# The second expert layer with its paired row blocks computed transposed, 256 tokens at a time

## The chip, the cores and the metric

The kernel runs on one core of one Trainium2 chip. The metric is the device time of one execution in microseconds (us), as the median of several runs. TensorE (PE in the profile) does the matrix products, ScalarE (ACT) and VectorE (DVE) read and write on-chip tiles elementwise, GpSimd (POOL) issues the gathers and scatters of rows, and SyncE (SP) issues the other transfers.

## What is computed

Attention with a window of 128 and 4 sink keys feeds two mixtures of experts. The change lies in the second one, cut here from the reference:

```python
logits = x @ w_gate                        # x 1536 x 512, 8 experts
expert_idx = np.argmax(logits, axis=1)
gate_w = softmax(logits)[arange(N), expert_idx]
for e in range(E):
    mask = expert_idx == e
    xe = x[mask]
    h = np.maximum(xe @ w1[e], 0.0)        # w1[e] 512 x 1024
    ye = h @ w2[e]                         # w2[e] 1024 x 512
    out[mask] = gate_w[mask, None] * ye
```

Every row goes to one expert, which is known only at run time. All products are made of parts: a number is split into a rounded high part and the remainder (low part), and one product is the sum of three matmuls, low x high, high x low, high x high (`mm3`, L66).

## The kernel before

Attention and the first mixture come first. The second mixture is cut into **items**, each a block of rows of one expert, numbered in the order in which they run. Items 0 and 1 are the two blocks of the fullest expert; they run while the tables for the others are still being made. Then follow 16 items: five **pairs** (3,4), (6,7), (9,10), (12,13), (15,16), two blocks of 128 rows of the same expert, and six **singles** 2, 5, 8, 11, 14, 17, of another expert each. Item 2 has 128 rows; singles 5 to 17 have 64 rows at most (`HALF`), put with their low parts side by side into 128 columns so that two matmuls do instead of three (`mm`, L768).

An item needs four weight tiles of 1 MB: halves 0 and 1 of the first layer (`w1`) and of the second (`w2`). A pair shares its four. So there are 11 x 4 = 44 tiles after item 1. Each is loaded by SP into one of four raw buffers and **split** in two pieces (`w_split`, L163): per piece ScalarE rounds 128x1024 elements into the high part (L175) and VectorE subtracts (L177). The split tiles go round seven slots (`SLOTS`, L136: wha0, wha1, xh0, xh1, xh2, whb0, whb1 and the same with l for the low parts) in the order of `SEQ` (L127): first layer of an item, second layer of the item before it, and so on. `spend(n)` (L849) writes n pieces into the program where it is called, if a slot is free; `ensure` (L863) writes what is still missing of a tile right before the matmuls that use it; `used` (L868) marks a slot free.

What an item i does:

- `gather(i)`: POOL fetches its rows by index. `xs_trans(i)` (L750): four transposes on PE, then the high part by ScalarE and the low part by VectorE.
- `m2_l1(i, hf)` (L781), the first layer's half hf: activations stationary, 512 weight columns moving, so the result has rows on the partitions. 12 matmuls of 512 columns a half (8 for a `HALF` item), then the result goes out through the rectifier (ScalarE for half 0, VectorE for half 1). A `HALF` item sums its two parts there (`both`, L776: a copy on ScalarE, an addition on VectorE).
- `h_trans(i)` (L800): eight transposes on PE turn the hidden layer, so that it can be stationary in the second layer; ScalarE makes the high part (L819) and VectorE the low part (L820).
- `m2_l2(i)` (L823): 24 matmuls of 512 columns (16 for a `HALF` item), then scaling by the gate on ScalarE (L840; for a `HALF` item `both` comes ahead of it) and a scatter of rows by POOL (L841).

The order is written out by hand in the loop at L1510: the first layer of item i+1 (with `gather` and `xs_trans` of later items), then the second layer of item i, with `h_trans(i+1)` in its middle. Each engine works off its own list in order; an instruction that waits holds what stands behind it.

Tiles of earlier stages are used again by name (`hand_over`, L1446): `acc0` to `acc11` were the accumulators of the first mixture, `hh0`, `hl0` and so on its hidden tiles.

Of the kernel before, what the change touches and what calls it, by code (L numbers as in the profile page):

```python
# [8 lines left out]
F32 = mybir.dt.float32  # L9
F32R = mybir.dt.float32r  # L10
# [13 lines left out]
def kernel(  # L24
# [62 lines left out]
    x2d = dram.tile([N, DM], F32, name="x2d")  # L87

    accp = ctx.enter_context(tc.tile_pool(name="accp", bufs=1))
    acc = [accp.tile([128, DM], F32, name=f"acc{i}") for i in range(NT)]  # L90
    xp = ctx.enter_context(tc.tile_pool(name="xp", bufs=1))
    hp_a = ctx.enter_context(tc.tile_pool(name="hp_a", bufs=1))
    xh = [xp.tile([128, KD, CH], F32R, name=f"xh{c}") for c in range(NC)]
# [24 lines left out]
    for t in range(NOVER):  # L118
        for j in range(2):
            FIRST[NSURE + 2 * t + j] = NSURE + 2 * t  # L120
            COL[NSURE + 2 * t + j] = 2 * t + j
    HALF = {2 + 3 * u for u in range(1, NONE)}

    def whose(i, rs):
        return [(i, r) for r in rs] if FIRST[i] == i else []
# [606 lines left out]
    def rows(i):  # L732
        return 64 if i in HALF else 128

# [7 lines left out]
    def gather(i):  # L742
# [4 lines left out]
        )  # L747
        xs_t[i] = x

    def xs_trans(i):  # L750
        x = xs_t.pop(i)
        n = rows(i)
        tp = pools["ps"].tile([128, KD, 128], F32, name="xst", tag="m0")[:, :, 0:n]
        for kk in range(KD):
            nc.tensor.transpose(tp[:, kk, :], x[0:n, kk * 128:(kk + 1) * 128], ident[0:n, 0:n])
        if i in HALF:

            st = stile("xsh", i, [128, KD, 128], F32R)
            nc.scalar.activation(st[:, :, 0:n], tp, AF.Copy)
            nc.vector.tensor_tensor(st[:, :, n:128], tp, st[:, :, 0:n].bitcast(F32), op=ALU.subtract)  # L760
            xst[i] = st, None
            return
        th = stile("xsh", i, [128, KD, 128], F32R)
        tl = stile("xsl", i, [128, KD, 128], F32R)
        nc.scalar.activation(th, tp, AF.Copy)
        nc.vector.tensor_tensor(tl, tp, th.bitcast(F32), op=ALU.subtract)
        xst[i] = th, tl

    def mm(out_ap, ah, al, bh, bl, start, stop):
        if al is not None:  # L770
            mm3(out_ap, ah, al, bh, bl, start, stop)
        else:
            nc.tensor.matmul(out_ap, ah, bl, start=start, stop=False)
            nc.tensor.matmul(out_ap, ah, bh, start=False, stop=stop)

    def both(dst, ps):  # L776

        nc.scalar.activation(dst, ps[64:128, :], AF.Copy)
        nc.vector.tensor_tensor(dst, ps[0:64, :], dst, op=ALU.add)

    def m2_l1(i, hf):  # L781
        if 2 <= i < NSURE:
            ensure(i, hf)
        th, tl = xst[i]
        wh, wl = w_t[pos[i, hf]]
        ps = ps_m.tile([128, HF], F32, name="L", tag=f"L{hf}")
        for kk in range(KD):
            a = None if tl is None else tl[:, kk, :]
            mm(ps, th[:, kk, :], a, wh[:, kk, :], wl[:, kk, :], kk == 0, kk == KD - 1)
            yield  # L790
        used(i, (hf,))
        h = h2[i, hf] = stile(f"h{hf}", i, [128, HF])
        if i in HALF:
            both(h[0:64, :], ps)
        elif hf == 0 or i < 2 or i == NSURE - 1:
            nc.scalar.activation(h, ps, AF.Relu)
        else:
            nc.vector.tensor_scalar(h, ps, 0.0, None, op0=ALU.max)

    def h_trans(i, hfs=(0, 1)):  # L800
        if hfs[0] == 0:
            h2t[i] = []
        for hf in hfs:
            n = rows(i)
            tp = pools["ps"].tile([128, FB, 128], F32, name="h2p", tag=f"y{1 + hf}")[:, :, 0:n]
            h = h2.pop((i, hf))
            for f in range(FB):
                nc.tensor.transpose(tp[:, f, :], h[0:n, f * 128:(f + 1) * 128], ident[0:n, 0:n])
            th = stile(f"hh{hf}", i, [128, FB, 128], F32R)
            if i in HALF:  # L810
                hi = th[:, :, 0:n]
                nc.scalar.activation(hi, tp, AF.Relu)
                nc.vector.scalar_tensor_tensor(
                    th[:, :, n:128], tp, 0.0, hi.bitcast(F32), op0=ALU.max, op1=ALU.subtract
                )
                h2t[i].append((th, None))
                continue
            tl = stile(f"hl{hf}", i, [128, FB, 128], F32R)
            nc.scalar.activation(th, tp, AF.Copy)  # L819
            nc.vector.tensor_tensor(tl, tp, th.bitcast(F32), op=ALU.subtract)  # L820
            h2t[i].append((th, tl))

    def m2_l2(i):  # L823
        pool, tag = ((ps_m, "y0"), (pools["ps"], "m2"))[i % 2]
        ps = pool.tile([128, DM], F32, name="y", tag=tag)
        for f in range(2 * FB):
            if f % FB == 0 and 2 <= i < NSURE:
                ensure(i, 2 + f // FB)
            th, tl = h2t[i][f // FB]
            wh, wl = w_t[pos[i, 2 + f // FB]]  # L830
            a = None if tl is None else tl[:, f % FB, :]
            mm(ps, th[:, f % FB, :], a, wh[:, f % FB, :], wl[:, f % FB, :], f == 0, f == 2 * FB - 1)
            if f % FB == FB - 1:
                used(i, (2 + f // FB,))
            yield
        y = stile("y", i, [128, DM])[0:rows(i), :]
        if i in HALF:
            both(y, ps)
            ps = y
        nc.scalar.activation(y, ps, AF.Copy, scale=index(g_s, g_d, i))  # L840
        nc.gpsimd.indirect_dma_start(  # L841
            out=out, out_offset=bass.IndirectOffsetOnAxis(ap=index(is_s, is_d, i), axis=0), in_=y, in_offset=None,
            bounds_check=N - 1, oob_is_err=False,
        )
# [4 lines left out]
    def spend(n):  # L849
        while n > 0:  # L850
            if not todo:
                m = head[0]
                if m >= NHEAD or (m >= len(SLOTS) and uses[m - len(SLOTS)] > 0):
                    return
                todo.append(item_split(m))
                head[0] += 1
            try:
                next(todo[0])
                n -= 1
            except StopIteration:  # L860
                todo.pop(0)
# [523 lines left out]
    def tick():  # L1385
        for job in list(jobs):
            job[0] -= 1
            if job[0] <= 0:
                try:
                    w = next(job[1])  # L1390
                    job[0] = 4 if w is None else w
                except StopIteration:
                    jobs.remove(job)

    with tc.manual_schedule():
# [50 lines left out]
        def hand_over():  # L1446
            raw2.extend(p.tile([128, FB, 512], F32, name="raw", tag="raw") for p in (raw_a, raw_b, raw_c, raw_c))
            s0 = (NG - 1) * NC * FB
            hs = [((hp_a if j < 4 else hp_b), j) for j in ((s0 + t) % 6 for t in range(6))]
            free = [(p, f"h{x}{j}") for p, j in hs for x in "hl"]  # L1450
            a = [(accp, f"acc{j}") for j in range(NT)]
            small.update(xs=[a[0], a[1], a[8]], xsh=a[3:5], xsl=a[5:7], R=[a[2], a[7]], y=a[9:11])
            small.update(h0=free[8:12:2], h1=free[9:12:2])
            for j, key in enumerate(("hh0", "hl0", "hh1", "hl1")):
                small[key] = [free[j], free[4 + j]]

        for g in range(NG):
            for c in range(NC):
# [23 lines left out]
        def mix(gen):  # L1482
            for _ in gen:
                tick()
# [5 lines left out]
        for i in range(2):  # L1490
            mix(m2_l1(i, 0))
            for n, _ in enumerate(m2_l1(i, 1)):
                tick()
                if n == 0:
                    h_trans(i, (0,))
            h_trans(i, (1,))
            for n, _ in enumerate(m2_l2(i)):
                tick()
                if n == 5:
                    while i + 1 not in xs_t:  # L1500
                        tick()
                    xs_trans(i + 1)
        mix(m2_l1(2, 0))
        xs_trans(3)
        mix(m2_l1(2, 1))
        while jobs:
            tick()
        h_trans(2)
        spend(4)
        for i in range(2, NSURE):  # L1510
            if i + 1 < NSURE:
                drain(m2_l1(i + 1, 0))
            if i + 3 < NSURE:
                gather(i + 3)
            spend(2 if i % 3 == 0 else 1)
            if i + 1 < NSURE:
                drain(m2_l1(i + 1, 1))
            spend(2)
            if i + 2 < NSURE:
                xs_trans(i + 2)  # L1520
            spend(1)
            for n, _ in enumerate(m2_l2(i)):
                if n == 4 and i + 1 < NSURE:
                    h_trans(i + 1)
            spend(1 if i < NSURE - 2 else 8)
        more = nc.values_load(mo_i[0:1, 0:1], min_val=0, max_val=NOVER)  # L1526

        def over(t):
# [53 lines left out]
```

## Time and profile before

| | us |
|---|---|
| median of 3 runs | 1449.45 (1448.16 to 1450.91) |
| the profiled execution | 1447.51 |
| its span, first to last instruction | 1445.3 |
| mean granted TensorE clock over the span | 0.996 of full speed |
| PE busy | 1406.3 (97%) |
| DVE busy | 684.6 (47%) |
| ACT busy | 454.1 (31%) |
| 16 items after item 1, from the first gather of L745 with `ig_d` to the last scatter | 1248.0 to 1438.8 |

The profiled execution took 2.2 us more than its span, for what lies around the first and the last instruction. Matmuls overlap: the duration of one in the profile (390 ns for 512 columns) is longer than the distance from the start of one to the start of the next, so distances between starts are what counts on PE.

### The profile page before, as it was taken

The numbers are of one execution on the slowest core, as the hardware profiler recorded it, in microseconds if no ns is written. First come the engines' busy times: TensorE is split into PE (matmuls) and PEld (weight loads), VectorE is DVE, ScalarE is ACT, GpSimd is POOL, SyncE is SP. The second block draws the span as 40 slices with busy tenths as digits, with TensorE's granted clock in tenths as the row PEclk, the third lists the DMA queues.
The fourth block names the chain that finished last, engine by engine and source line by source line (L and its number), as shares of the span: only waits on it lengthen the run. The fifth ranks groups of instructions, "written<-read, shape, count | busy, mean of one in ns | idle before, by whom it ended". The sixth has DMA issues, their size and how long they took to land. (4 is left out here: it accounts for less than half of the span.)

```text
span 1445.3 us, 17989 instructions
## 1 busy us (share of the span) xinstructions
PE 1406.3 (97%) x7101; PEld 1150.3 (80%) x7101; DVE 684.6 (47%) x1369; ACT 454.1 (31%) x895; POOL 130.2 (9%) x172
## 2 busy tenths in 40 slices
PE   7799999999999999999999999999999999899997
PEld 5587887888888888888888888888888877688885
DVE  7777644543333323232433333242323257877884
ACT  5766522021121112020221112020221123477774
POOL 3644400000000000000000000000000000212221
PEclk9999999999999999999999999999999999999999
DMA  6322112010101000010101000010100041797782
GB/s 131 78 59 53 38 59 87 1 59 1 59 0 59 29 29 30 29 59 0 58 0 59 30 30 30 30 58 0 58 1 0 15 161 37 248 319 276 271 291 71
DMA packets 85707, 105.01 MB, mean 73 GB/s; under 512 B 41358, under 2 KB 41358, under 8 KB 85616
## 3 DMA queue, kind: packets, MB, share of 16 engines
q1 hardware_dynamic: 83056, 96.58, 20.2%
q0 software_dynamic: 2560, 7.21, 1.4%
q8 instruction: 58, 0.95, 0.3%
q14 instruction: 33, 0.27, 0.1%
HBM read 100.63 MB, written 7.21 MB: 75 GB/s over the span
## 5 line engine op out<-in xcount | busy, mean ns | idle before, releaser
L210 ACT ACTIVATE hh<-L 128x512 fp32r<-128x512 f32 x192 | 114.7, 597 | 794.9 <-PE L L69 794.8
L211 DVE SCALAR_TENSOR_TENSOR hl<-L,hh 128x512 fp32r<-128x512 f32 x192 | 132.8, 692 | 345.5 <-ACT hh L210 344.8
L235 DVE SCALAR_TENSOR_TENSOR acc<-y,Pm,acc 128x512 f32<-128x512 f32 x168 | 126.1, 751 | 252.3 <-PE y L69 251.9
L67 PE MATMUL y<-whb,hl 128*128 128x512 f32 x416 | 164.8, 396 | 0.0
L67 PE MATMUL y<-wha,hl 128*128 128x512 f32 x412 | 163.2, 396 | 0.0
L69 PE MATMUL y<-whb,hh 128*128 128x512 f32 x416 | 162.2, 390 | 0.0
L68 PE MATMUL y<-wlb,hh 128*128 128x512 f32 x416 | 162.1, 390 | 0.0
L69 PE MATMUL y<-wha,hh 128*128 128x512 f32 x412 | 160.6, 390 | 0.0
L68 PE MATMUL y<-wla,hh 128*128 128x512 f32 x412 | 160.5, 390 | 0.0
L67 PE MATMUL L<-xh,wla 128*128 128x512 f32 x384 | 152.2, 396 | 0.0
L67 PE MATMUL L<-xh,wlb 128*128 128x512 f32 x384 | 150.9, 393 | 0.0
L68 PE MATMUL L<-xl,wha 128*128 128x512 f32 x384 | 149.6, 389 | 0.0
L69 PE MATMUL L<-xh,wha 128*128 128x512 f32 x384 | 149.6, 389 | 0.0
L68 PE MATMUL L<-xl,whb 128*128 128x512 f32 x384 | 149.5, 389 | 0.0
L69 PE MATMUL L<-xh,whb 128*128 128x512 f32 x384 | 149.5, 389 | 0.0
L745 POOL DMA_INDIRECT acc<-x2d,ig_s x2 | 2.1, 1048 | 1044.2 <-DVE tmp_d L458 1019.1
L69 PEld LDWEIGHTS y<-whb,hh 128*128 128x128 f32 x416 | 78.1, 188 | 16.6
L67 PEld LDWEIGHTS y<-whb,hl 128*128 128x128 f32 x416 | 78.1, 188 | 15.7
L67 PEld LDWEIGHTS y<-wha,hl 128*128 128x128 f32 x412 | 77.3, 188 | 16.5 <-issue 0.2
L68 PEld LDWEIGHTS y<-wlb,hh 128*128 128x128 f32 x416 | 78.2, 188 | 15.3
L69 PEld LDWEIGHTS y<-wha,hh 128*128 128x128 f32 x412 | 77.3, 188 | 16.3
L68 PEld LDWEIGHTS y<-wla,hh 128*128 128x128 f32 x412 | 77.4, 188 | 14.8
(346 smaller groups left out, 2297.0 us busy)
## 6 DMA issues: line engine op xcount, KB each, us to landing
raw<-in_moe_w SPq DMA_DIRECT2D x80, 1024.0 KB
raw<-in_v SPq DMA_DIRECT2D x12, 256.0 KB
raw<-vfb SPq DMA_DIRECT2D x12, 256.0 KB
x2d<-acc SPq DMA_DIRECT2D x12, 256.0 KB
raw<-in_k SPq DMA_DIRECT2D x11, 256.0 KB
raw<-in_q SPq DMA_DIRECT2D x11, 256.0 KB
raw<-in_k SPq DMA_DIRECT2D x2, 128.0 KB
raw<-in_q SPq DMA_DIRECT2D x2, 128.0 KB
```

The costliest lines, as they stand in the source:

```text
L67: nc.tensor.matmul(out_ap, al, bh, start=start, stop=False)
L68: nc.tensor.matmul(out_ap, ah, bl, start=False, stop=False)
L69: nc.tensor.matmul(out_ap, ah, bh, start=False, stop=stop)
L210: nc.scalar.activation(hh, ps, AF.Relu)
L211: nc.vector.scalar_tensor_tensor(hl, ps, 0.0, hh.bitcast(F32), op0=ALU.max, op1=ALU.subtract)
L235: nc.vector.scalar_tensor_tensor(a, ps, Pm[:, blk, e:e + 1], a, op0=ALU.mult, op1=ALU.add)
L745: nc.gpsimd.indirect_dma_start(out=x[0:rows(i), :], out_offset=None, in_=src, in_offset=bass.IndirectOffsetOnAxis(ap=index(ig_s, ig_d, i), ...
```

## The change

The first layer of a pair is computed once for both blocks, with the weights stationary and 256 tokens moving (`pair_l1`). The result has the hidden units on the partitions, so the pairs need no `h_trans`; the rectifier writes high and low parts from the accumulator directly. `xs_trans` writes the two blocks of a pair into one tile of 256 columns. Items are worked off by units, pair or single: the first layer of the next unit, then the second layer of this one. The places of `gather`, `xs_trans` and `spend` are written anew, and several tiles lie elsewhere: `acc3`/`acc4` and `acc5`/`acc6` are each one tile, the hidden tiles of singles have one buffer instead of two, and eight tiles (`hp`) hold a pair's hidden layer.

```diff
-    acc = [accp.tile([128, DM], F32, name=f"acc{i}") for i in range(NT)]
+    acc = [None if 3 <= i < 7 else accp.tile([128, DM], F32, name=f"acc{i}") for i in range(NT)]
+    for i in (3, 5):
+        t = accp.tile([128, 2, DM], F32, name=f"acc{i}")
+        acc[i], acc[i + 1] = t[:, 0, :], t[:, 1, :]
...
+    PAIR = {3 + 3 * t for t in range(NPAIR)}
...
     def xs_trans(i):
...
+        if i in PAIR:
+            xpair[i] = [stile("xp", j, [128, KD, 256], F32R) for j in range(2)]
...
+        if i in PAIR or i - 1 in PAIR:
+            js = slice(0, 128) if i in PAIR else slice(128, 256)
+            th, tl = (t[:, :, js] for t in xpair[i if i in PAIR else i - 1])
+            nc.scalar.activation(th, tp, AF.Copy)
+            nc.vector.tensor_tensor(tl, tp, th.bitcast(F32), op=ALU.subtract)
+            return
...
+    def pair_l1(i, hf):
+
+        ensure(i, hf)
+        th, tl = xpair[i]
+        wh, wl = w_t[pos[i, hf]]
+        for u in range(2):
+            ps = ps_m.tile([128, 2, 256], F32, name="L", tag=f"L{u}")
+            for j in range(2):
+                fs = slice((2 * u + j) * 128, (2 * u + j + 1) * 128)
+                for kk in range(KD):
+                    mm3(ps[:, j, :], wh[:, kk, fs], wl[:, kk, fs], th[:, kk, :], tl[:, kk, :], kk == 0, kk == KD - 1)
+            if u == 1:
+                used(i, (hf,))
+                used(i + 1, (hf,))
+            n = 2 * (2 * hf + u)
+            hh, hl = (stile("hp", n + j, [128, 2, 256], F32R) for j in range(2))
+            nc.scalar.activation(hh, ps, AF.Relu)
+            nc.vector.scalar_tensor_tensor(hl, ps, 0.0, hh.bitcast(F32), op0=ALU.max, op1=ALU.subtract)
+            for b in range(2):
+                for j in range(2):
+                    h2t.setdefault(i + b, []).append(
+                        (hh[:, j, b * 128:(b + 1) * 128], hl[:, j, b * 128:(b + 1) * 128])
+                    )
+            yield
...
-            small.update(xs=[a[0], a[1], a[8]], xsh=a[3:5], xsl=a[5:7], R=[a[2], a[7]], y=a[9:11])
-            small.update(h0=free[8:12:2], h1=free[9:12:2])
+            small.update(xs=[a[0], a[1], a[8]], xsh=[a[3], a[3], a[11]], xsl=[a[5], a[5], (pools["s"], "x2h")], R=[a[2], a[7]])
+            small.update(y=a[9:11], h0=free[8:9], h1=free[9:10], xp=[a[3], a[5]])
+            small.update(hp=free[4:8] + free[10:12] + [a[2], a[7]])
             for j, key in enumerate(("hh0", "hl0", "hh1", "hl1")):
-                small[key] = [free[j], free[4 + j]]
+                small[key] = [free[j]]
...
+        def turn(i):
+
+            xs_trans(i)
+            if i + 3 < NSURE:
+                gather(i + 3)
+
+        gather(5)
         mix(m2_l1(2, 0))
-        xs_trans(3)
+        turn(3)
         mix(m2_l1(2, 1))
         while jobs:
             tick()
+        turn(4)
         h_trans(2)
-        spend(4)
-        for i in range(2, NSURE):
-            if i + 1 < NSURE:
-                drain(m2_l1(i + 1, 0))
-            if i + 3 < NSURE:
-                gather(i + 3)
-            spend(2 if i % 3 == 0 else 1)
-            if i + 1 < NSURE:
-                drain(m2_l1(i + 1, 1))
-            spend(2)
-            if i + 2 < NSURE:
-                xs_trans(i + 2)
-            spend(1)
-            for n, _ in enumerate(m2_l2(i)):
-                if n == 4 and i + 1 < NSURE:
-                    h_trans(i + 1)
-            spend(1 if i < NSURE - 2 else 8)
+        spend(3)
+        units = [(2,)]
+        for i in sorted(PAIR):
+            units += [(i, i + 1), (i + 2,)]
+        for n, u in enumerate(units):
+            v, w = (units[n + k] if n + k < len(units) else () for k in (1, 2))
+            for hf in range(2):
+                if len(v) == 2:
+                    for k, _ in enumerate(pair_l1(v[0], hf)):
+                        spend(2 - k)
+                elif v:
+                    drain(m2_l1(v[0], hf))
+                    spend(1)
+                for i in w[hf:hf + 1]:
+                    turn(i)
+            for i in u:
+                for k, _ in enumerate(m2_l2(i)):
+                    if k == 4 and i == u[-1] and len(v) == 1:
+                        h_trans(v[0])
+                    if k % 3 == 2:
+                        spend(1)
+            if n == len(units) - 2:
+                spend(8)
```

How the order moves, shown at the third pair (9,10) and the single 11 behind it; the other rounds read alike. First ScalarE's list before, from the output of single 8 to the hidden layer of single 11 (L778 is the copy in `both`, L840 the gate, L175 a split piece, L796 the rectifier, L759 a turned block of 64 rows, L819 the turned hidden layer):

```order
L778 ACTIVATE acc9_11160<-y_11125 64x512 [waits DMASW0_49,PE_49,Activation_49]
L840 ACTIVATE acc9_11160<-acc9_11160,g_d_3203 64x512 [waits DVE_49]
L175 ACTIVATE whb1_11121<-raw_9388 128x1024
L796 ACTIVATE hh4_11182<-L_11169 128x512 [waits PE_49]
L175 ACTIVATE wha0_11187<-raw_9385 128x1024 [waits DMAHW2_49]
L175 ACTIVATE wha0_11187<-raw_9385 128x1024
L175 ACTIVATE wha1_11209<-raw_9386 128x1024 [waits DMAHW3_49,Activation_49]
L175 ACTIVATE wha1_11209<-raw_9386 128x1024
L759 ACTIVATE acc4_11220<-xst_11215 128x4x64 [waits PE_49,Activation_49]
L175 ACTIVATE xh0_11224<-raw_9387 128x1024 [waits DMAHW4_49]
L819 ACTIVATE hh0_11249<-h2p_11244 128x512 [waits PE_49,Activation_49]
```

The weights of single 11's first layer are wha0 and wha1. Between their pieces and the matmuls that use them, PE has the rest of item 10's first layer and the second layer of item 9. Now the same engine after the change (L812 is the rectifier of a pair's quarter, L793 the copy in `both`, L879 the gate, L180 a split piece, L768 a turned block of a pair):

```order
L812 ACTIVATE acc2_11253<-L_11228 128x512 [waits PE_49]
L180 ACTIVATE whb1_11224<-raw_9386 128x1024
L180 ACTIVATE wha0_11267<-raw_9383 128x1024 [waits DMAHW2_49,DVE_49]
L180 ACTIVATE wha0_11267<-raw_9383 128x1024
L793 ACTIVATE acc9_11283<-y_11259 64x512 [waits DMASW4_49,PE_49,Activation_49]
L879 ACTIVATE acc9_11283<-acc9_11283,g_d_3201 64x512 [waits DVE_49]
L180 ACTIVATE wha1_11291<-raw_9384 128x1024 [waits DMAHW3_49]
L793 ACTIVATE hh4_11304<-L_11295 64x512 [waits PE_49]
L180 ACTIVATE wha1_11291<-raw_9384 128x1024
L768 ACTIVATE acc3_11309<-xst_11311 128x4x128 [waits PE_49]
```

The two pieces of wha1 now stand behind single 8's output (whose gate waits for VectorE), and the second of them behind the first half of single 11's own hidden layer. And PE's list there after the change, from the last matmul of single 8's second layer (y_11259) to single 11's first layer in two halves (L_11295, L_11325):

```order
L789 MATMUL y_11259<-xh2_11132,hh1_11073 128x512
L788 MATMUL L_11295<-wla0_11268,acc11_11177 128x512 [waits DVE_49,PE_49]
L789 MATMUL L_11295<-wha0_11267,acc11_11177 128x512 [waits Activation_49]
...
L764 MATMUL xst_11311<-ident_69,acc0_10972 128x128 [waits DMASW2_49]
L764 MATMUL xst_11311<-ident_69,acc0_10972 128x128 x3
L788 MATMUL L_11325<-wla1_11292,acc11_11177 128x512 [waits DVE_49,PE_49]
L789 MATMUL L_11325<-wha1_11291,acc11_11177 128x512 [waits Activation_49]
L788 MATMUL L_11325<-wla1_11292,acc11_11177 128x512
L789 MATMUL L_11325<-wha1_11291,acc11_11177 128x512
L788 MATMUL L_11325<-wla1_11292,acc11_11177 128x512 [waits DVE_49]
L789 MATMUL L_11325<-wha1_11291,acc11_11177 128x512 [waits Activation_49]
```

Single 11's first layer now follows single 8's second layer at once; before, items 9 and 10 lay between. Its second half waits for VectorE twice, once for each piece of wha1.

## Rows read from the trace of the kernel before

**Rows 1.** Stretches: us, busy of PE, PEld, DVE, ACT, POOL, PEclk, DMA share, GB/s.
```profile
1280.00:1300.00 20.00, 20.00 (x101) 16.10 (x100) 15.15 (x18) 13.50 (x20) 2.60 (x3) 1.00 0.88 301
...
1380.00:1400.00 20.00, 20.00 (x101) 16.09 (x101) 16.84 (x20) 14.96 (x22) 4.01 (x3) 1.00 0.89 303
```

**Rows 2.** Waits, 1240 to 1446 us: who for whom, total us, times, longest.
```profile
PEld L L67 <- DVE acc L766: 0.5, 1, 0.5
```

**Rows 3.** POOL's timeline: the scatters of items 4 and 7; start us, us.
```profile
1300.23 1.01 POOL L841 DMA_INDIRECT out<-acc,is_d  x1 [7.69 <-ACT acc L840]
...
1333.50 1.01 POOL L841 DMA_INDIRECT out<-acc,is_d  x1 [7.64 <-ACT acc L840]
```

**Rows 4.** PE's timeline in item 2's second layer, item 3's transposes in its middle.
```profile
1272.99 0.39 PE L69 MATMUL y<-xh,hh 128*128 128x512 f32 x1
1273.22 0.60 PE L808 MATMUL h2p<-ident,hh 128*128 128x128 f32 x4
1273.65 0.60 PE L808 MATMUL h2p<-ident,hl 128*128 128x128 f32 x4
1274.01 0.47 PE L67 MATMUL y<-xh,hl 128*128 128x512 f32 x1
...
1276.17 0.39 PE L67 MATMUL L<-whb,acc 128*128 128x512 f32 x1
...
1281.16 0.39 PE L68 MATMUL L<-wla,acc 128*128 128x512 f32 x1
```

**Rows 5.** PE's timeline in attention: 64 stationary columns, 128 moving.
```profile
60.68 0.22 PE L67 MATMUL pv<-pt,vl 128*64 128x128 f32 x1
...
61.41 0.22 PE L1281 MATMUL pv<-skh,vsk 128*64 128x128 f32 x1
```

**Rows 6.** Groups by form, 1240 to 1446 us: xcount | busy, mean ns | idle.
```profile
L820 DVE TENSOR_TENSOR hl<-h2p,hh 128x512 fp32r<-128x512 f32 x24 | 15.6, 684 | 0.8 <-ACT hh L819 0.7
L819 ACT ACTIVATE hh<-h2p 128x512 fp32r<-128x512 f32 x24 | 13.3, 597 | 13.7 <-PE h2p L808 13.7
L798 DVE TENSOR_SCALAR hl<-L 128x512 f32<-128x512 f32 x11 | 7.5, 684 | 0.0
L796 ACT ACTIVATE hh<-L 128x512 f32<-128x512 f32 x12 | 7.2, 597 | 9.9 <-PE L L69 9.8
L69 PEld LDWEIGHTS L<-xh,acc 128*128 128x128 f32 x44 | 8.3, 188 | 1.7
```

**Rows 7.** The page's groups: the same two evictions in the first mixture.
```profile
L210 ACT ACTIVATE hh<-L 128x512 fp32r<-128x512 f32 x192 | 114.7, 597 | 794.9 <-PE L L69 794.8
L211 DVE SCALAR_TENSOR_TENSOR hl<-L,hh 128x512 fp32r<-128x512 f32 x192 | 132.8, 692 | 345.5 <-ACT hh L210 344.8
```

**Rows 8.** All engines' timeline behind single 14's second layer.
```profile
1409.12 1.28 DVE L820 TENSOR_TENSOR hl<-h2p,hh 128x512 fp32r<-128x512 f32 x2
1409.24 0.39 PE L67 MATMUL L<-xh,acc 128*128 128x512 f32 x1
1409.49 0.60 ACT L778 ACTIVATE acc<-y 64x512 f32<-64x512 f32 x1 [0.77 <-ACT hh L819]
1410.32 0.67 DVE L779 TENSOR_TENSOR acc<-y,acc 64x512 f32<-64x512 f32 x1
1411.03 0.73 ACT L840 ACTIVATE acc<-acc,g_d 64x512 f32<-64x512 f32 x1 [0.94 <-DVE acc L779]
1411.65 1.04 ACT L175 ACTIVATE wha<-raw 128x1024 fp32r<-128x1024 f32 x1
1412.72 0.60 ACT L796 ACTIVATE hh<-L 128x512 f32<-128x512 f32 x1
1412.73 1.23 DVE L177 TENSOR_TENSOR wla<-raw,wha 128x1024 fp32r<-128x1024 f32 x1 [1.74 <-ACT wha L175]
1413.22 2.94 ACT L175 ACTIVATE xh<-raw 128x1024 fp32r<-128x1024 f32 x3
1414.30 2.36 DVE L177 TENSOR_TENSOR xl<-raw,xh 128x1024 fp32r<-128x1024 f32 x2 [0.34 <-ACT xh L175]
```

More of the change, by code (lines that the diff above doesn't have):

```diff
@@ L748, in gather @@
         xs_t[i] = x
+    xpair = {}
     def xs_trans(i):
@@ L815, in h_trans @@
                 )
-                h2t[i].append((th, None))
+                h2t[i] += [(th[:, f, :], None) for f in range(FB)]
                 continue
@@ L820, in h_trans @@
             nc.vector.tensor_tensor(tl, tp, th.bitcast(F32), op=ALU.subtract)
-            h2t[i].append((th, tl))
+            h2t[i] += [(th[:, f, :], tl[:, f, :]) for f in range(FB)]
     def m2_l2(i):
@@ L828, in m2_l2 @@
                 ensure(i, 2 + f // FB)
-            th, tl = h2t[i][f // FB]
+            th, tl = h2t[i][f]
             wh, wl = w_t[pos[i, 2 + f // FB]]
-            a = None if tl is None else tl[:, f % FB, :]
-            mm(ps, th[:, f % FB, :], a, wh[:, f % FB, :], wl[:, f % FB, :], f == 0, f == 2 * FB - 1)
+            mm(ps, th, tl, wh[:, f % FB, :], wl[:, f % FB, :], f == 0, f == 2 * FB - 1)
             if f % FB == FB - 1:
```

## The prediction

> **What bounds the kernel now.** I read the stretches first. In the items' stage PE is busy in every 20 us of 20 at full granted clock, while ACT and DVE work 13 to 17 and the DMA engines move about 300 GB/s at a share of 0.88 to 0.89 [rows 1]. So this stage is PE's, and what PE issues sets its time. The list of waits confirms it: from 1240 us to the end PE stands for a split or an eviction of first-layer operands only once, for 0.5 us [rows 2]; no weight tile is ever late. One round (a pair and a single) is read from the scatters of the last item of two successive pairs: 33.27 us [rows 3]. The rest of the kernel, until the fullest expert's two items, keeps its work; there the change only renames tiles, and a write to one half of a joined accumulator waits for the same engine as before.
>
> **What PE loses.** A pair's blocks need no h_trans. In rows 4 eight transposes stand between two matmuls of the second layer. From the start of the matmul ahead of them (1272.99) to the tenth matmul after it (1276.17) go 3.18 us. Ten matmuls of 512 columns take 2.27 at 0.227 each, which is the distance over the 22 that follow, 4.99 us [rows 4]. So one h_trans costs 0.91 us, with the slow restart behind it. Ten of them go: **-9.1 us**, all on PE's path. With them go 20 evictions each on ACT (L819) and DVE (L820), and 10 rectifiers on each (L796, L798); 20 of each come in their place, of the form that the first mixture has [rows 6, 7]. ACT is relieved of 6.0 us (30 x 0.597 less 20 x 0.597), DVE of 6.7 (30 x 0.684 less 20 x 0.692). Neither was on the path, so I count nothing for that by itself.
>
> **What PE gets instead.** The first layer of a pair was 48 matmuls of 512 columns, 10.9 us, and becomes 96 of 256, each with its own weight load of 128 columns. No row shows that form. Half of 227 ns is 113.5. The nearest row is attention's product of 64 stationary and 128 moving columns, half of the new form in both: 12 steps from 60.68 to 61.41 us, 61 ns each [rows 5]. Twice that is 122. A straight line through 128 columns at 61 and 512 at 227 gives 116 for 256, and I take that: 480 x (116.3 - 113.4) = **+1.4 us**, between 0 and 4.1.
>
> The Trainium skill, "TensorE: Matmul & The Clock Gate", section "Back-to-back issue gap", gives 81 ns for 128 columns and 131 for 512 for a stream of load and matmul pairs, so that short matmuls are dear. By a line through those, an estimate, 256 columns take 98, and the change would cost 480 x 98 - 240 x 131 = +15.6 us instead of +1.4. Rows 4 and 5 disagree with both figures, and the measurement decides.
>
> **The wait that comes in.** The new order moves the first layer of a single from behind the first block of the pair's second layer to ahead of it, so its weights are wanted 5.4 us earlier in the round, but the splits are not written earlier. ACT's list shows it: the two pieces of the tile for the single's second half stand behind the previous single's output, and the second piece also behind the first half of the hidden layer. PE's list has both waits. I work out one round from the end of the previous single's second layer, called 0.
>
> PE wants the second half's tile after 8 matmuls (1.82) and a block's four transposes with restart (about 0.49: in rows 4 eight take 0.91), so at 2.31. The chain that delivers its first piece already stands in the trace, behind single 14, where its piece is not wanted so soon [rows 8]: PE is done with the output at 1409.24, ACT copies at 1409.49, DVE adds at 1410.32, ACT scales at 1411.03 and splits at 1411.65, DVE subtracts at 1412.73 and ends at 1413.96. That is 4.72 us, so PE waits 2.4. It then has 4 matmuls (0.91), until 5.63. For the second piece ACT copies the hidden layer and splits again. A split piece in a series takes ACT 0.95 (2.94 less 1.04, over 2) and DVE 1.13 (2.36 less 1.23), a 128x512 eviction 0.50 and 0.60 [rows 8]. So ACT starts piece one at 2.41, the copy at 3.36, piece two at 3.86 and ends at 4.9; DVE ends piece one at 4.63, adds until 5.23, and ends piece two at 6.45. PE waits another 0.8. Together 3.2.
>
> To this comes a queue on DVE. In the last 6.35 us ahead of 0 (the last quarter of the pair's first layer, 2.72, and 16 matmuls, 3.63) the list gives DVE two evictions and five split pieces, 2 x 0.60 + 5 x 1.13 = 6.9 us of work. It can start when ACT has rectified the third quarter, at about -5.5, waits 0.35 for ACT once, and is through at 1.75. The addition of the output would be ready for it at 0.9. So the chain is 0.85 later, and the wait is **4.0 us** a round, between 3.2 and, with the longer pair, 4.1.
>
> Four singles have this. For single 17 no block is turned in between, so PE is there 0.49 earlier: 4.5. For single 5 only the second piece is late, since both others stand ahead of item 2's output: ACT copies the hidden layer at 2.07, splits from 2.57 to 3.6, DVE ends at 4.9, and PE wants it at 3.2: 1.7. Sum 1.7 + 3 x 4.0 + 4.5 = **+18.2 us**. While PE stands, nothing else gains: the next things ACT and DVE have to do follow from PE's work.
>
> Moved steps at no cost: the gathers stand ahead of the scatter in POOL's list and are issued a round ahead of their transposes; a load into a raw buffer waits for DVE's subtraction four tiles earlier, by the same timetable some 10 us ahead of the split that needs it; item 4's transposes stand before item 2's h_trans, and fall in a gap there. If a load came late, it would add to the same wait.
>
> **The sum.** -9.1 + 1.4 + 18.2 = +10.5 on the profiled execution of 1447.5, so 1458.0. The median of the runs is 1.9 above that execution, so about **1460**. With the low ends (no queue on DVE, no dearer matmul): -9.1 + 15.0 = +5.9, 1455. With the high end of the matmul: +13.2, 1463. This case has 74 in 100.
>
> **Rivals.**
> 1. *The splits are covered.* ACT gets to the single's second tile before the output has to be written, or the evictions are quicker than I chain them; then only the transposes count: -9.1 + 1.4 = -7.7, **1442**. For it: ACT and DVE lose 6 us of work and idle 3 to 7 us in each 20 [rows 1]. Against: the order of ACT's list is fixed, and the chain is one that the trace has. It decides when the waits sum to less than 7.7 us, some 1.6 per single. 13 in 100.
> 2. *The waits are half of what I chain,* because the evictions of PE's results start sooner than in rows 8: 0.8 + 3 x 2.0 + 2.3 = 9.1, so +1.4, **1451**. 9 in 100.
> 3. *The weight load sets the pace of the short matmuls.* A load of 128 columns lasts 188 ns in the trace [rows 6]; if the next can't start sooner, 480 x (188 - 113.4) = +35.8, and with 15.0 of waits **1491**. Against it: in attention a load of half that size keeps a pace of 61 ns [rows 5]. 4 in 100. The page named above states that both operations set the spacing; rows 5 bear that out only as far as 61 ns.
>
> That the change does not do what it says is excluded: PE's list has the 480 matmuls of 256 columns and the transposes of the singles alone.
>
> **How the numbers follow.** A measurement of this kernel tells about 0.2%, 2.9 us, from no change. Slower: the forecast and rival 3, 0.78. The same: rival 2, 0.09. Faster: rival 1, 0.13. The range is 1450 to 1464: it holds the forecast's own 1455 to 1463 and rival 2, and leaves out rivals 1 and 3 and a little beyond.
>
> **What would show it.** In the profile after: pair matmuls 113 to 122 ns apart; h2p transposes for the six singles and the two items ahead alone; a round some 2 us longer than 33.27; and in the list of waits PE or its weight loads standing for DVE's split of a first-layer tile, about 2 and 1 us in four rounds, in front of a single's second half. I am wrong if PE has no such waits there, or if a round is 31 to 32 us.

## The result, and the profile after

The changed kernel takes **1465.18 us** (median of 4 runs, 1464.6 to 1467.22), the kernel before 1449.51 beside it (4 runs, 1448.16 to 1450.91): a ratio of 1.0115, 95% interval 1.0104 to 1.0127. The profiled execution took 1464.6 us, 17.1 us more than that of before, with a span of 1462.7; its granted clock is 0.990 of full speed (0.996 before). The forecast was slower, at 1460 within 1450 to 1464; the time lies 1.2 us above that range.

The stretches of the kernel after, columns as in [rows 1]:

```profile
1300.00:1320.00 20.00, 19.52 (x133) 17.30 (x132) 14.02 (x15) 12.84 (x18) 2.29 (x3) 1.00 0.68 245
1320.00:1340.00 20.00, 17.52 (x96) 14.54 (x96) 12.67 (x14) 11.61 (x17) 5.20 (x5) 1.00 0.83 278
1340.00:1360.00 20.00, 17.04 (x109) 14.52 (x108) 16.23 (x18) 15.45 (x20) 3.93 (x4) 0.98 0.79 274
1360.00:1380.00 20.00, 20.00 (x112) 17.16 (x111) 11.06 (x13) 10.47 (x14) 2.98 (x3) 0.93 0.76 255
1380.00:1400.00 20.00, 17.03 (x95) 14.10 (x94) 16.00 (x19) 13.98 (x19) 2.17 (x2) 0.92 0.72 252
```

Where PE was busy in 20 of 20 us [rows 1], it now stands for up to 3 us of them. The second thing is in the column behind POOL's: the granted clock is below 1.00 from the third of these stretches on. Every stretch of [rows 1] has 1.00.

PE's list of waits from 1240 us on has three rows of waits for a split of weights, a kind that the list before lacks (it has 0.5 us for an eviction of first-layer operands [rows 2]):

```profile
PE L L788 <- DVE wla L182: 5.9, 6, 2.0
PE L L788 <- DVE xl L182: 5.9, 5, 2.5
PE L L788 <- DVE wlb L182: 2.1, 2, 1.6
```

L788 is the first layer of a single (`mm`), L182 VectorE's half of a split: 13.9 us in 13 waits. Nine of them stand in front of a single's second half, as the prediction said; the other four, of 0.5 us each, stand in front of the first half, where it had none.

A round is read here from the first transpose of each single's rows (64x64, L764), which stands between the two halves of a pair's first layer. PE's timeline of the kernel after:

```profile
1306.80 0.40 PE L764 MATMUL xst<-ident,acc 64*128 64x64 f32 x3
...
1342.72 0.46 PE L764 MATMUL xst<-ident,acc 64*128 64x64 f32 x4
...
1380.06 0.46 PE L764 MATMUL xst<-ident,acc 64*128 64x64 f32 x4
...
1417.50 0.27 PE L764 MATMUL xst<-ident,acc 64*128 64x64 f32 x1
```

The rounds last 35.92, 37.34 and 37.44 us, against 33.27 [rows 3]. The first of them is 2.65 longer, as forecast ("some 2 us"); the others are 1.4 to 1.5 us longer still, with the same work and the same waits. PE's timeline in front of single 11 shows both the waits and the difference:

```profile
1353.25 0.47 PE L788 MATMUL L<-wla,acc 128*128 128x512 f32 x1 [0.48 <-DVE wla L182]
...
1355.33 0.60 PE L764 MATMUL xst<-ident,acc 128*128 128x128 f32 x4
1357.94 0.47 PE L788 MATMUL L<-wla,acc 128*128 128x512 f32 x1 [2.02 <-DVE wla L182]
1358.25 0.39 PE L789 MATMUL L<-wha,acc 128*128 128x512 f32 x1
...
1359.58 0.80 PE L788 MATMUL L<-wla,acc 128*128 128x512 f32 x1 [0.47 <-DVE wla L182]
1360.17 0.63 PE L789 MATMUL L<-wha,acc 128*128 128x512 f32 x1
1360.60 0.63 PE L788 MATMUL L<-wla,acc 128*128 128x512 f32 x1
1361.02 0.63 PE L789 MATMUL L<-wha,acc 128*128 128x512 f32 x1
```

The waits stand in front of the first half (0.48) and of both pieces of the second half (2.02 and 0.47). Behind them matmuls of 512 columns follow each other at 0.43 us instead of 0.23. The stretches of one microsecond, with the columns of [rows 1], give the reason:

```profile
1358.00:1359.00 1.00, 1.00 (x4) 0.58 (x4) 1.00 (x2) 1.00 (x2) 0.66 (x1) 1.00 0.99 375
1359.00:1360.00 1.00, 0.53 (x2) 0.43 (x2) 1.00 (x2) 0.54 (x1) 0.00 (x0) 0.61 0.79 201
1360.00:1361.00 1.00, 1.00 (x3) 0.73 (x3) 1.00 (x2) 0.00 (x0) 0.00 (x0) 0.50 0.86 143
1361.00:1362.00 1.00, 1.00 (x5) 0.77 (x4) 0.25 (x1) 0.31 (x1) 0.00 (x0) 0.50 0.57 111
1362.00:1363.00 1.00, 1.00 (x6) 0.90 (x5) 0.68 (x1) 1.00 (x2) 0.22 (x1) 0.69 1.04 391
```

The granted clock goes from 1.00 (2.4 GHz) to 0.50 (1.2 GHz) for 3.41 us, from 1359.21 to 1362.62, after PE had stood 2.02 us; a second wait, of 0.47, falls into it. The trace has three such stretches in the items' stage, behind the waits of singles 11, 14 and 17; behind those of single 8, in the round before, there is none. The kernel before has none in this stage until 1438.5 us, its end. So about 4.4 us of the loss is neither work nor a wait, and the prediction has no term for it.

What the waits wait for, in the timeline of all engines of the kernel after (rows of the other engines left out):

```profile
1351.89 2.36 DVE L182 TENSOR_TENSOR wla<-raw,wha 128x1024 fp32r<-128x1024 f32 x2
...
1352.86 0.59 ACT L793 ACTIVATE acc<-y 64x512 f32<-64x512 f32 x1 [0.26 <-ACT wha L180]
...
1354.16 0.68 DVE L794 TENSOR_TENSOR acc<-y,acc 64x512 f32<-64x512 f32 x1
...
1354.87 0.73 ACT L879 ACTIVATE acc<-acc,g_d 64x512 f32<-64x512 f32 x1 [1.41 <-DVE acc L794]
...
1355.50 1.04 ACT L180 ACTIVATE wha<-raw 128x1024 fp32r<-128x1024 f32 x1
...
1356.57 1.22 DVE L182 TENSOR_TENSOR wla<-raw,wha 128x1024 fp32r<-128x1024 f32 x1 [1.74 <-ACT wha L180]
```

This is the chain of [rows 8] with its queue: the addition L794 stands behind two splits on DVE, ACT's scaling L879 waits 1.41 us for it, and the split that PE wants stands behind the scaling. That one ends at 1357.79, and PE goes on at 1357.94.

The form that no row of before showed, in PE's timeline of the kernel after:

```profile
1302.75 0.28 PE L67 MATMUL L<-acc,wla 128*128 128x256 f32 x1
...
1306.59 0.28 PE L69 MATMUL L<-acc,wha 128*128 128x256 f32 x1
```

These are 32 steps, 3.84 us: 120 ns each. Over all 470 distances of this form in the stage the mean is 122.1 ns.

### The profile page after: what moved, and what is told of

It is laid out like the page before. It is cut to its first block, busy times and chain, and to the rows that moved or that the text cites. A ratio compares the mean times of both kernels' runs of the same rounds, so it can differ in the third digit from the quotient of the medians.

```text
span 1462.7 us, 18232 instructions
## 1 busy us (share of the span) xinstructions
PE 1411.0 (96%) x7261; PEld 1159.7 (79%) x7261; DVE 680.2 (47%) x1359; ACT 449.7 (31%) x885; POOL 127.1 (9%) x172
## 5 line engine op out<-in xcount | busy, mean ns | idle before, releaser
L67 PE MATMUL y<-whb,hl 128*128 128x512 f32 x408 | 161.7, 396 | 0.0
L67 PE MATMUL y<-wha,hl 128*128 128x512 f32 x404 | 160.0, 396 | 0.0
L68 PE MATMUL y<-wlb,hh 128*128 128x512 f32 x408 | 158.9, 390 | 0.0
L69 PE MATMUL y<-whb,hh 128*128 128x512 f32 x408 | 158.9, 390 | 0.0
L69 PE MATMUL y<-wha,hh 128*128 128x512 f32 x404 | 157.6, 390 | 0.0
L69 PEld LDWEIGHTS y<-whb,hh 128*128 128x128 f32 x408 | 76.6, 188 | 16.3
L67 PEld LDWEIGHTS y<-wha,hl 128*128 128x128 f32 x404 | 76.1, 188 | 16.3 <-issue 0.5
```

The lines of the kernel that those rows point to most:

```text
L67: nc.tensor.matmul(out_ap, al, bh, start=start, stop=False)
L68: nc.tensor.matmul(out_ap, ah, bl, start=False, stop=False)
```

## The experiments

Two theories of the waits stood at the start: that the splits are only asked for too late, so that asking earlier ends them; and that ScalarE and VectorE are too crowded around a single, so that a wait comes back elsewhere. For the half clock there was one suspicion: that it falls because PE stands still.

**Splits asked for earlier.**

```diff
-                        spend(2 - k)
+                        spend(2)
```

> Edit: the changed kernel, with two split pieces after every quarter of a pair's first layer instead of two and one, so that both tiles of the next single's first layer are split before the previous single's output is written. Theory A (PE waits because those pieces stand behind the output in ScalarE's and VectorE's lists, and the clock falls because PE waits): no wait above 0.3 us in front of the second half of a single's first layer, no stretch at half clock in the items' stage, and what is left is -9.1 us of transposes and +4.2 us of 256-column matmuls: about 1445 us. Rival B (VectorE has too much to do in a pair's first layer, so the wait only moves): waits of 2 us and more stand somewhere else in each round, 1455 to 1465 us. Rival C (the clock falls for the 256-column matmuls themselves): half-clock stretches stay, about 1450 us.

1460.05 us (1457.5 to 1462.72), ratio 1.0069, 1.0052 to 1.0085. The time is the one that Rival B named, and so is what happened: the waits in front of the singles are gone, and in the rounds behind the first one of 3.2 us stands in another place. The timeline of all engines of this kernel:

```profile
1361.74 1.04 ACT L180 ACTIVATE xh<-raw 128x1024 fp32r<-128x1024 f32 x1
...
1362.81 0.60 ACT L768 ACTIVATE acc<-xst 128x512 fp32r<-128x512 f32 x1
1362.82 1.23 DVE L182 TENSOR_TENSOR xl<-raw,xh 128x1024 fp32r<-128x1024 f32 x1 [0.26 <-ACT xh L180]
...
1363.96 0.68 DVE L769 TENSOR_TENSOR acc<-xst,acc 128x512 fp32r<-128x512 f32 x1
...
1364.70 0.47 PE L764 MATMUL xst<-ident,acc 128*128 128x128 f32 x2 [3.19 <-DVE acc L769]
```

The transposes of a pair's second block want the one PSUM bank (`m0`) that the first block's transposes filled. It is read by L768 and L769, and each of these stands behind a split. So the wait moved, and with it the half clock: three stretches of 3.41 us in the pairs' rounds, from 1327.43, 1364.98 and 1402.53. What this run leaves open is whether the bank or the crowded engines are to blame.

**The single's first layer back between the pair's second layers,** with the transposed activations kept:

```diff
             for i in u:
+                if i == u[-1]:
+                    first()
```

(`first()` is the block of first layers that stood ahead of this loop.)

> Edit: the changed kernel, with a single's first layer put back between the second layers of the two blocks of the pair, as before the change; the number of split pieces written at each place stays. Theory A: the tiles of the single have 5.4 us more, the output of the previous single is long out, and there are no waits: about 1445 us, as with the earlier split. If the number of pieces were the cause and not the order, the waits stay at about 3 us a round and the time at 1460 to 1465 us. Rival C (clock): half-clock stretches stay without waits, about 1450 us.

1453.25 us (7 runs, 1451.66 to 1454.59), ratio 1.003, 1.0018 to 1.0041. Behind the first, the rounds are 33.84, 34.03 and 33.99 us long, by the same mark as above. PE still waits for splits (L788 for `xl` 3.1 us in 4 waits, for `wla` 2.8 in 3), and only one stretch at half clock is left. The order is worth 12 us, but it is not all: the time lies between what Theory A expected (1445) and what was named for the number of pieces (1460 to 1465).

**PE kept at work in the wait:** eight matmuls of 512 columns whose result nobody reads, ahead of the second half of each single's first layer.

```diff
+                if len(v) == 1 and hf == 0:
+                    fill(v[0])
```

> Edit: the changed kernel with eight more matmuls of 512 columns, whose result nobody reads, ahead of the second half of each single's first layer: 1.8 us of PE work in a wait of 2.0 us (2.6 for the last single). If the clock falls because PE stands still there: no half-clock stretch in rounds 3, 4 and 5, and the time is 4 to 5 us below that of the changed kernel, about 1460.5 us, though PE does more. If the clock falls for another reason: the three half-clock stretches stay, 1465 us or up to 2 us more.

1460.42 us (1459.52 to 1461.41), ratio 1.0076, 1.0059 to 1.0093: with 40 matmuls more, 4.8 us faster than the change. PE's timeline of this kernel in front of single 11, and the stretches around it:

```profile
1356.46 2.10 PE L1562 MATMUL fill<-wha 128*128 128x512 f32 x8
1358.72 0.47 PE L788 MATMUL L<-wla,acc 128*128 128x512 f32 x1 [0.16 <-DVE wla L182]
1359.03 0.39 PE L789 MATMUL L<-wha,acc 128*128 128x512 f32 x1
```

```profile
1340.00:1360.00 20.00, 19.24 (x122) 16.27 (x121) 15.45 (x17) 15.16 (x20) 4.72 (x4) 1.00 0.82 282
1360.00:1380.00 20.00, 19.64 (x117) 16.94 (x118) 12.46 (x15) 11.22 (x16) 2.96 (x3) 1.00 0.81 264
```

The dummy work fills 2.1 us that PE would have stood, the real work starts no earlier, and the clock stays at 1.00: no stretch at half clock in the items' stage (the last one before its end, from 1231.58 us, lies ahead of it). The rounds are 35.93, 35.95 and 35.94 us, all as long as the one undisturbed round of the change. So the clock fell because PE stood, and its price was some 1.5 us a time, 4.8 in all. The Trainium skill, "TensorE: Matmul & The Clock Gate", section "HAM oscillation — how this bites in real kernels", describes a matmul kernel that loses clock where PE waits for its loads; this pair of runs agrees in kind, with waits for splits in their place, which at 2.0 us are shorter than the page's.

**Moved columns cut to 128:** the order of the second experiment, each matmul of 256 columns made of two of 128.

```diff
-                for kk in range(KD):
-                    mm3(ps[:, j, :], wh[:, kk, fs], wl[:, kk, fs], th[:, kk, :], tl[:, kk, :], kk == 0, kk == KD - 1)
+                for b in range(2):
+                    bs = slice(b * 128, (b + 1) * 128)
+                    for kk in range(KD):
+                        mm3(ps[:, j, bs], wh[:, kk, fs], wl[:, kk, fs], th[:, kk, bs], tl[:, kk, bs], kk == 0, kk == KD - 1)
```

> Edit: the kernel with the single's first layer between the pair's second layers, and each 256-column matmul of a pair cut into two of 128 columns with the same stationary weights loaded twice. If the weight load of 128 columns sets the pace of the 256-column matmuls (122 ns): 128-column matmuls are also 110 to 122 ns apart, 960 of them take 47 to 59 us more than the same work at half that pace, and the time is 1490 to 1505 us. If the columns and a fixed part set it, as in attention (61 ns for 128 columns with 64 stationary): 61 to 66 ns apart, within 5 us of the kernel that it is made from, about 1447 us.

1500.47 us (one run), 47 us above the second experiment and in the range named for a pace that the load sets. PE's timeline of this kernel:

```profile
1316.06 0.27 PE L67 MATMUL L<-acc,wla 128*128 128x128 f32 x1
...
1317.07 0.28 PE L67 MATMUL L<-acc,wla 128*128 128x128 f32 x1
```

Nine steps in 1.01 us: 112 ns, for half the columns of a step that takes 122. So something other than the moving columns sets a pace of 112 ns here. It goes with the stationary side: attention's 128 moving columns on 64 stationary ones go at 61 ns [rows 5]. A load lasts 188 ns in the profile of before [rows 6] and 192 in this one, and yet loads start 112 ns apart here. That it is the load that sets the pace is the likeliest reading; these two rows are all that it rests on. The Trainium skill, "TensorE: Matmul & The Clock Gate", section "LDWEIGHTS (loading the stationary operand)", gives a load a time in proportion to its columns; by its formula 128 columns make 107 ns, an estimate, to which the 112 ns come close.

**Bank and splits taken apart.** Three kernels, and a fourth further below. The two edits are the one of the first experiment (two split pieces for every quarter) and a second bank:

```diff
-        tp = pools["ps"].tile([128, KD, 128], F32, name="xst", tag="m0")[:, :, 0:n]
+        tp = pools["ps"].tile([128, KD, 128], F32, name="xst", tag=f"m{i % 2 if i > 2 else 0}")[:, :, 0:n]
```

Both edits, in the order of the second experiment (the fifth kernel):

> The single block's first layer stands between the pair's two second layers, the splits are asked for two a quarter, and the blocks' transposes take two PSUM banks in turn. Theory A (all of the loss behind the ten matmul quarters is one wait that moves from place to place: for splits asked for late, else for the one bank of the transposes): with both taken away the round is 33.27 - 1.82 + 0.83 = 32.28 us and five rounds are some 5 us shorter than before, 1443 to 1446 us, with no stretch at half clock in the items' stage. Theory B (VectorE and ScalarE can't deliver the splits of a pair in time in any order, because evictions of the pair come in lumps): waits of 1.5 to 2 us a round stay and the time is that of the run with the single between, 1451 to 1454 us.

1442.87 us (5 runs, 1441.24 to 1446.11), ratio 0.9961, 0.9947 to 0.9974: faster than before. From the pairs on PE waits for no split and no bank, and the rounds behind the first are 32.05, 32.04 and 32.05 us (32.28 expected). Theory A holds; one stretch at half clock is left, ahead of the pairs.

Both edits, in the order of the change (the sixth kernel):

> As the run with splits asked for two a quarter (1460.05 us), and the blocks' transposes take two PSUM banks in turn; the order of the change is kept. Theory A (the wait moved there to the one bank, behind an eviction that VectorE had queued after the splits): the transposes of the pair's second block no longer wait for the eviction of the first, the three waits of 3.2 us and the three stretches at half clock go, 1444 to 1449 us. Theory B (the bank is only where the lateness shows; the matmuls after it need the splits that are late): the wait moves to the first layer of the pair or the second of the single, 1455 to 1461 us.

1442.4 us (4 runs, 1441.24 to 1443.92), ratio **0.9954**, 0.9939 to 0.9969. PE's timeline and the stretches of this kernel:

```profile
1306.66 0.40 PE L764 MATMUL xst<-ident,acc 64*128 64x64 f32 x3
...
1338.71 0.46 PE L764 MATMUL xst<-ident,acc 64*128 64x64 f32 x4
...
1370.76 0.46 PE L764 MATMUL xst<-ident,acc 64*128 64x64 f32 x4
...
1402.80 0.40 PE L764 MATMUL xst<-ident,acc 64*128 64x64 f32 x3
```

```profile
1320.00:1340.00 20.00, 20.00 (x123) 17.35 (x122) 13.39 (x16) 14.30 (x20) 8.23 (x6) 1.00 0.81 276
1340.00:1360.00 20.00, 20.00 (x114) 17.41 (x113) 18.31 (x21) 16.99 (x23) 3.80 (x5) 1.00 0.96 333
```

Rounds of 32.05, 32.05 and 32.04 us, PE busy throughout at full clock, although ACT and DVE are busier in these stretches than in those of the change. It is a little below what Theory A expected (1444 to 1449): the engines were never too slow for the splits, only their lists were in the wrong order and the transposes one bank short. That the same time comes out in both orders shows that with both edits the order no longer matters.

Splits asked for early, one bank, single between (the seventh kernel):

> The single between the pair's second layers and two splits a quarter, one PSUM bank for the transposes. Theory A (the order decides): the transposes of the pair's second block have other work of TensorE between them and the first block's, the bank is free by then, 1444 to 1448 us, the same as with two banks. Theory B (the bank decides): some 3 us a round of wait at the second block's transposes as in the run with early splits, 1453 to 1460 us.

1447.51 us (10 runs, 1446.84 to 1450.04), ratio 0.9993, 0.9984 to 1.0002, no difference from before. That is within what Theory A expected, but not the same as with two banks: the other work between the two blocks' transposes covers most of the wait for the bank, not all. PE's timeline has the rest, once in each of four rounds, and the rounds are 33.47 us:

```profile
1328.69 0.66 PE L764 MATMUL xst<-ident,acc 128*128 128x128 f32 x4 [1.21 <-DVE acc L769]
```

**The pair's first layer with 512 columns again** (the eighth kernel), into the same tiles and otherwise as the fifth, which the expectation below calls the first of these runs; it leaves out that the activations come out transposed.

```diff
-            for j in range(2):
-                fs = slice((2 * u + j) * 128, (2 * u + j + 1) * 128)
-                for kk in range(KD):
-                    mm3(ps[:, j, :], wh[:, kk, fs], wl[:, kk, fs], th[:, kk, :], tl[:, kk, :], kk == 0, kk == KD - 1)
+            us = slice(u * 128, (u + 1) * 128)
+            for kk in range(KD):
+                mm3(ps, th[:, kk, us], tl[:, kk, us], wh[:, kk, :], wl[:, kk, :], kk == 0, kk == KD - 1)
```

> The first of these runs with the pair's first layer computed with tokens stationary and 512 weight columns moving, into the same tiles: what it leaves out is the transposition of the activations, so the second layer multiplies wrongly placed numbers; all waits, evictions and splits stay. 240 matmuls of 512 columns (227 ns) stand where 480 of 256 (122.1 ns) stood. Theory A (the 256-column matmuls cost 4 us over the five pairs by their pace alone): 4 us less than the first of these runs. Theory B (the pace is hidden by waits that close up): under 1.5 us less.

1438.79 us (4 runs, 1438.41 to 1440.34), 4.1 below the fifth kernel in the median and 2.8 in the fastest runs (1441.24 and 1438.41). PE's timeline of this kernel:

```profile
1303.27 0.39 PE L764 MATMUL xst<-ident,acc 64*128 64x64 f32 x3
...
1334.76 0.46 PE L764 MATMUL xst<-ident,acc 64*128 64x64 f32 x4
...
1366.24 0.46 PE L764 MATMUL xst<-ident,acc 64*128 64x64 f32 x4
```

Its rounds are 31.49 and 31.48 us, 0.56 less than 32.05; five make 2.8. The rest of the 4.1 is not the pace: two of the fifth kernel's five runs take 1446.1 us, and the one of them that was profiled has stretches at half clock that this kernel's has not, two in attention and one from 1259.12, behind a wait for a gather. So the 256 columns cost 2.8 us, between what the two theories gave (4, and under 1.5). The 4 took 227 ns for the matmuls of 512 columns. In a round of this kernel the two halves, which stand behind transposes, take 5.54 and 5.61 us for 24 of them (from 1297.73 and 1303.65 us), 231 and 234 ns each; in the fifth they take 5.83 and 5.85 for 48 of 256 columns.

This run also prices the transposes: without them, and with 512 columns as before, a round is 33.27 - 31.49 = 1.78 us shorter. The order differs too, so this is the net of both.

**The second bank alone** (the ninth kernel), in the order of the change:

> The changed kernel with only the blocks' transposes in two PSUM banks in turn; the splits are asked for as late as in the change. Theory A (two causes in a row: the late splits hold the singles' first layer, and only where they are early does the one bank hold the next round): the bank by itself is worth nothing, 1462 to 1467 us with the same waits for splits and the same stretches at half clock in rounds 3 to 5. Theory B (the one bank holds VectorE's queue as well, and so makes the splits late): the waits for splits shrink to half, 1450 to 1457 us.

1466.17 us (4 runs, 1464.25 to 1468.11), ratio 1.0122, 1.0103 to 1.0142, as the change, with its waits (L788 for `wla` 5.9 us in 6, for `xl` 5.9 in 5) and its three stretches at half clock. Theory A: two causes in a row. The four kernels in the change's order, medians in us:

| | one bank | two banks |
|---|---|---|
| splits as in the change | 1465.18 | 1466.17 |
| two split pieces a quarter | 1460.05 | 1442.4 |

Either edit by itself is worth 5 us at most, both together 23. The first wait hides the second.

## Why the prediction was wrong by a little and right in the main

**The transposes, -9.1: right.** Measured 1.78 us a round for two h_trans, forecast 1.82; five rounds make -8.9.

**The matmuls of 256 columns, +1.4: too low by half.** In place they cost 0.56 us a round, 2.8 in all. The term was mis-sized by the straight line through 128 columns at 61 ns and 512 at 227: its lower point has only 64 stationary columns, and the run with 128 moving columns shows 112 ns with 128 stationary ones. The line had no right to that point. The 122 ns that the prediction set aside as its upper bound, twice the 61, is what came out.

**The waits, +18.2: right in size, and in place but for the four short ones.** Against the rounds of the kernel without waits they are 35.92 - 32.05 = 3.87 us for single 8 (forecast 4.0). Single 5 lies in the round before these: 35.73 against 33.85 in that kernel (from 1271.07 and 1272.81), 1.9 (forecast 1.7). For single 17, from the last single's transposes to the last scatter, 1417.50 to 1454.95 against 1402.80 to 1434.30: 5.95 longer, and 4.5 without a stretch at half clock of about 1.47 (forecast 4.5). With 3.87 for each of 8, 11 and 14 the sum is 18.0. The list's 13.9 us are less: a matmul's 0.39 us overlap the next one's by some 0.16, and the first two starts behind a wait lie 0.31 us apart (1357.94 and 1358.25), so that from start to start more is lost than PE stands idle. That makes some 0.24 us a wait, 3.1 of the 4.1 between the two; the rest is not taken apart here. One detail differs: PE also waited 0.48 us ahead of the first half, which I had in time, and then less ahead of the second, 2.02 and 0.47 us, where I had 2.4 and 0.8 and the queue's 0.85. The 0.85 was counted from 0.9, where the addition of the output is ready; in the chain of [rows 8] it starts 1.08 behind PE's end (1410.32 less 1409.24), so by its own rows the queue was worth 0.67.

**What was missing, +4.4.** "While PE stands, nothing else gains" ended the part on the waits, and the sum counted a wait at its own length, with the matmuls behind it at full clock. That is the step that failed: it put the clock at nothing. Behind the waits the clock was granted at half for 3.41 us in three rounds. The rounds lengthen by 1.42 and 1.52 by it; with 1.47 for the third they make 4.4, and the run with filler gave 4.8 back. With 2.8 in place of 1.4 alone the forecast would have been 1461.3; without the 4.4 the measured time would have been 1460.8, inside the range. The clock made the difference.

-8.9 + 2.8 + 18.0 + 4.4 = +16.3, of 17.1 between the profiled executions. The rest lies ahead of the stage, whose first gather is at 1248.9 instead of 1248.0 us, and the traces show where: the first matmul of the first mixture starts at 75.56 us instead of 74.63, and ten microseconds earlier attention's matmuls are only 0.07 us later than before. The stretch between, after and then before:

```profile
60.00:80.00 20.00, 16.77 (x157) 13.59 (x157) 13.58 (x45) 14.03 (x40) 14.28 (x17) 0.91 0.24 54
60.00:80.00 20.00, 16.33 (x170) 13.27 (x171) 14.85 (x48) 14.72 (x42) 14.16 (x17) 1.00 0.24 55
```

The execution after has 3.41 us at half clock there, from 65.56, and the one before has not. How much of attention runs at half clock differs between the profiled executions: in the nine experiments, whose attention is that of the change, the same matmul starts 0.5 to 3.0 us later than before. So these 0.9 us say little about the change; no run tells whether it has a part in them.

**The rivals.** That the splits are covered (1442) didn't happen, but it is the time of the kernel with both edits, 1442.4: the condition named for it, waits of under 1.6 us a single, is what the two edits bring about. That the figures agree so closely is partly chance, since its -7.7 are -6.1 in the rounds (five times 33.27 - 32.05). Its argument, that ACT and DVE have time to spare, was right; the order of their lists stood against it. Waits of half the size (1451) and a pace of 188 ns (1491) didn't come; of the latter's mechanism the fourth kernel shows a pace of 112 ns that the moving columns do not set, under the 122 of this form. The 188 ns is the duration of a load, and loads of 192 ns started 112 ns apart there.

**Better than both kernels** is the changed one with two split pieces for every quarter and a second bank for the blocks' transposes: 0.9954 of before, 0.9939 to 0.9969. Of its gain of 6.5 us five rounds of 33.27 - 32.05 = 1.22 make 6.1.

## What to carry to other kernels

When an order is changed so that a step wants its operands earlier, move the work that makes them too, all of it: the transposes gained 9 us here and late splits took 18. Behind the first wait look for the next, since either of two edits was worth little by itself and both together 23 us. Price a wait of PE at more than its length where it is microseconds long, and check the granted clock behind it; and take the pace of a small matmul from rows with the same stationary columns, not only the same moving ones.

## What the runs showed of the hardware

- The clock of PE was granted at half (1.2 GHz) for 3.41 us at a time, from the end of a wait or shortly behind it, with PE busy again. Filling 2.1 us of each single's wait with matmuls that nobody reads kept it at 2.4 GHz in the stage and made the kernel 4.8 us faster. What decides whether a wait brings it on stays open: single 8's waits did not, singles 11 and 14's, of the same length, did, and so did single 17's; and a wait of some 2 us for a gather, which these kernels have near 1255 us, brought it in the profiled executions of the first, fifth, sixth and seventh kernels of the experiments (2.08 to 2.35 us) and in no other (1.80 to 2.08 us).
- With 128 stationary columns matmuls of these parts follow each other at 112 ns for 128 moving columns, 120 to 122 for 256 and 227 for 512. At 112 ns for half the columns nothing is gained below 256: cutting them to 128, in twice as many matmuls, cost 47 us.
